# Second DFT stage of a long convolution: 128x128 products with a block-diagonal matrix, or 64x64 products on the four parts of the array

## The chip, the cores and the metric

The kernel runs on one core of a Trainium2 chip. TensorE (PE in the profile) multiplies, VectorE (DVE), ScalarE (ACT) and GpSimd (POOL) work on tiles, SyncE (SP) issues transfers. The metric is the device time of one execution in microseconds; the median of three runs before the change is 216.64 us (216.44 to 218.06).

## What is computed

`x` is `A_q`, 2048 positions of 640 channels. Cut to what matters:

```python
xn = layernorm(x)
k_shift = sum over t of k shifted by t, times shift_k       # 4 taps
kv = k_shift * v
y  = irfft(rfft(kv padded to 4096) * rfft(ssm_k padded to 4096))[:2048]
y  = y + kv * ssm_D
s  = xn * y
g  = silu(gelu(xn @ w1 + b1) @ w2 + b2)                     # 640 -> 1728 -> 640
out = x + s * g
```

So there are two branches: a causal convolution of length 2048 in each of 640 channels, with a filter of its own, and a dense layer pair. Both use the normalized `x`, and they meet in a product.

## The kernel before

**The convolution** is done by a DFT in two stages, both as products on TensorE. Position s is 16 p + n, with p on the 128 partitions and n = 0 to 15. Stage one (`k_f1` for the filter, `u_f1` for kv) multiplies, for each n, a table of 128 cosines or sines by the 128x640 tile of that n; the result, 128 lines of real and 128 of imaginary parts, is copied from PSUM to SBUF and stored to scratch in HBM (scrK, scrU; GpSimd's queue). Read back in another order (SyncE's queue), 32 groups of 128 lines each arise. A group holds four frequencies r; for each it has 16 values of n, each with a real and an imaginary line. Stage two is a DFT over n: one constant 128x128 matrix, `F2m`, with four equal 32x32 blocks on its diagonal and zeros elsewhere. The filter goes through it in `k_f2` (steps `ff0` to `ff31` of the list), kv in `u_f2` (`mu0` to `mu31`).

`product` (`mp`, L532) is VectorE's: it multiplies a kv group, read straight from PSUM, by the filter's group and by the same group with its real and imaginary lines exchanged (`swap_load`, a transfer from SBUF to SBUF). The inverse of stage two, `inv1` (`mc`, L541 and L542), multiplies these two results by the constant matrices `I1a` and `I1b`, both with the same four diagonal blocks' places, and adds them in PSUM. The result is copied out (`me`), stored to scrC (`ms`), read back (`yl`), and goes through the inverse of stage one (`y`, L573); then come the gate, the addition of `x` and the store.

A product of a group is two matmuls of 320 columns each, since a bank of PSUM holds 512 floats: `mm2` (L196) writes the halves of the 640 channels to two neighbouring banks. `mm2` serves both stages; the trace tells them apart by the operand (`mats` is stage two). Copies out of PSUM are `evac`, on ScalarE (L190) or VectorE (L191).

**The dense layers** (`ffn1`, L439, steps `h` and `ha`/`hb`; `ffn2`, L454, steps `g`) run over four chunks of 512 positions. They depend only on `x`, and are laid between the convolution's steps.

**The order** is written out by hand, or by a planner outside the kernel: `PLAN` is a list of 957 words, and the kernel issues them one by one, in the order of each engine. A word gives the step, the row of the shared SBUF tile `mem` after "/", the PSUM banks after "@" (all eight banks are handed out this way), and the engine of a copy after "~": `me2/74~a` copies inverse 2 to row 74 on ScalarE, `~d` means VectorE. No scheduler changes this order; a step waits until its operands are there, and all later steps of the same engine wait behind it.

Of the kernel before, what the change touches and what calls it, by code (L numbers as in the profile page):

```python
# [36 lines left out]
cm1_1/32 he0_1 h0_8@7 cm0_1/89 he0_13 he0_11 kl2 cm1_0/58 h0_7@1 kl3 he0_8 cm0_0/60 tt1_0@0 cm0_2/62 he0_7 xl2/91
g0_1@2 ca1_1 te1_0/0~d vl1/4 cm0_3/95 g0_0@3 ge0_1/0 ca0_1 vl2/97 d ca0_2 kt4@4 ge0_0/1 cm1_3/101 kt1@5 kc4/103~a
g0_2@2 vl3/104 gm0_0 kc1/108~a ca0_3 gm0_1 cm1_2/109 kt0@3 ge0_2/2 kt2@6 cv0 kc0/68~a kf1_0@0.1 kf1_1@4.5 ke1_0/66~a
g0_5@7 gm0_2 kc2/65~d ke1_1~a ca1_2 ks1 cm2_0/32 kf0_0@2.3 ge0_5/1 kt7@6 cm2_1/34 ke0_0/89~a kf0_1@0.1 kf2_1@4.5  # L40
cm2_2/62 kt3@7 ke0_1~a kf2_0@2.3 kc3/64~d ks0 kf4_1@0.1 ke2_0/36~a kc7/95~d kt5@7 ke2_1~a ca2_1 kf4_0@2.3 g0_3@6
kc5/96~a ks2 gm0_5 cm2_3/28 ke4_0/108~a ke4_1~d kf5_1@4.5 ca2_2 ge0_3/0 kt6@7 ks4 kf3_0@2.3 kf5_0@0.1 gm0_3
ke3_0/34~a g0_6@6 cm3_1/65 ke5_0/67~a ca2_3 kc6/38~a ke5_1~d kt8@2 ge0_6/2 kf6_0@0.1 cv2 ks5 kf6_1@4.5 kf3_1@6.7
ke6_0/39~a kc8/110~d g0_4@3 ke3_1~d ke6_1~a cm3_0/62 ks3 ks6 cm3_2/89 uf0_0@0.1 ge0_4/1 uf0_1@6.7 tt1_1@2 ue0_0/28~a
ca1_3 uf1_1@4.5 tt1_2@3 ue0_1~a te1_1~d uf1_0@0.1 te1_2~a kf8_0@6.7 us0 cv1 g0_7@2 ue1_0/4~a ue1_1~d ke8_0/37~a
cm3_3/108 us1 uf2_0@0.1 gm0_6 ge0_7/0 uf2_1@4.5 gm0_4 uf3_0@6.7 ue2_0/101~a cm4_0/60 it1@3 ue3_0/67~a kt9@2 ue2_1~d
kf8_1@0.1 kc9/96~a kf7_0@6.7 ie1~d kf7_1@4.5 us2 ke7_0/30~a it2@2 ke8_1~d it3@3 ke7_1~a kf9_1@6.7 ie2/39~d ks8 ie3~a
kf9_0@0.1 uf3_1@4.5 st2_2 ks7 h1_0@2 ue3_1~a ke9_0/34~d us3 kt10@3 ke9_1~a uf4_0@4.5 kc10/36~d kt11@0 he1_0 ks9
ue4_0/28~d h1_1@1 kc11/64~d kf10_0@6.7 ca3_1 kf11_0@4.5 he1_1 h1_3@3 ke10_0/4~d ke11_0/95~a ca3_2 uf4_1@0.1 he1_3
uf5_0@6.7 kf10_1@4.5 cm4_3/58 ue4_1~a kt12@2 h1_6@3 ue5_0/101~a ca3_3 us4 kc12/103~a ke10_1~d kf11_1@0.1 uf5_1@6.7  # L50
he1_6 h1_2@2 ke11_1~d ks10 ue5_1~a cv3 ks11 kf12_0@4.5 he1_2 kf12_1@0.1 us5 kt13@3 ke12_0/37~d ke12_1~a uf6_1@6.7
h1_11@2 cm4_2/67 kc13/110~a ks12 cm4_1/65 kf13_0@4.5 he1_11 uf6_0@0.1 h1_4@3 ke13_0/89~d ue6_0/35~a ca4_1 ue6_1~a
kf13_1@4.5 uf7_0@0.1 he1_4 st2_3 us6 uf7_1@6.7 kt15@2 ke13_1~a h1_5@3 st2_0 kc15/34~a ks13 ue7_0/108~a h1_9@4 ca4_2
he1_5 st2_1 kf15_0@0.1 ue7_1~a kf15_1@2.3 kt14@5 ke15_0/32~a us7 h1_8@6 ca4_3 kc14/43~a rs2 ke15_1~d he1_9 h1_10@7
cv4 he1_8 kf14_0@0.1 he1_10 cm5_1/4 kf14_1@2.3 ks15 uf8_0@4.5 ke14_0/6~a h1_7@6 nm2_1 nm2_2 ke14_1~a nm2_0 uf8_1@0.1
nm2_3 he1_7 ks14 uf9_0@2.3 ue8_0/95~d h1_13@7 ue8_1~a ue9_0/101~d us8 tt2_2@6 he1_13 uf9_1@4.5 cm5_0/62 h1_12@0
ue9_1~a gm0_7 fl2/64 ca5_1 fl3/66 us9 tt2_0@1 he1_12 fl5/89 g1_1@7 cm5_2/37 fl0/58 te2_0/12~a fl15/16 cm5_3/18
fl14/20 te2_2~a ca5_2 g1_0@6 ge1_1/2 cm6_2/97 ca5_3 cm7_1/43 ff5@2.3 ge1_0/1 ff4@4.5 ff6@0.1 cv5 fl1/22 fe4/108~a
g1_6@7 fe5~a gm1_0 cm6_1/24 fe6/26~a mk2/60 cm6_0/28 uf10_0@4.5 ge1_6/0 uf10_1@2.3 cm7_0/6 uf11_0@0.1 ue10_0/30~a
g1_3@6 ue10_1~a ca6_1 ue11_0/95~a us10 ca7_1 ca6_2 uf11_1@4.5 ge1_3/1 ff2@2.3 ff3@0.1 ue11_1~a cm7_2/45 g1_5@7 fl6/0  # L60
fe2/2~a us11 cm6_3/4 fe3~a ca7_2 mk1/18 ff7@4.5 ca6_3 ff0@2.3 fe7~a ff1@0.1 g1_2@6 fl7/102 cm7_3/37 fe0/35~a fl4/33
mk3/64 cv6 fe1~a gm1_3 mk0/52 ca7_3 uf12_0@4.5 ge1_5/1 uf13_0@2.3 ue12_0/100~a uf12_1@0.1 st3_1 g1_4@7 ue13_0/24~a
cv7 ue12_1~a gm1_1 us12 gm1_5 uf15_0@4.5 ge1_2/2 st3_3 uf13_1@2.3 ge1_4/1 uf15_1@0.1 ue13_1~a tt2_1@6 ue15_0/22~d
g1_7@7 te2_1~a us13 gm1_2 st3_0 uf14_0@2.3 ue15_1~d ge1_7/2 uf14_1@4.5 h2_9@6 ue14_0/4~a st3_2 us15 ue14_1~a
ff12@0.1 he2_9 gm1_6 us14 ff8@2.3 gm1_4 ff28@4.5 fe12/58~d h2_7@7 rs3 fe28/37~d h2_0@0 fe8/62~a gm1_7 he2_7 ml1/104
nm3_3 ff10@4.5 ml7/106 nm3_0 ff30@2.3 he2_0 ff9@6.7 nm3_2 ml3/95 h2_12@1 fe30/28~a fe10/30~d ml0/97 ml2/43 fe9~a
nm3_1 fl9/45 ff14@2.3 he2_12 ff31@4.5 ml5/47 ff29@6.7 mk4/99 h2_8@0 fe14/49~a fe29~d fe31~a fl12/6 ff11@2.3 he2_8
q1/66 mu2@6.7 ff15@4.5 mp2/24 fe11~a h2_3@1 fl8/70 fe15~a mu7@2.3 he2_3 fl13/32 mu0@4.5 mp7/72 mc2@6.7 h2_1@0 mk5/22
me2/74~a mp0/4 mu6@6.7 mk7/76 he2_1 ff18@2.3 h2_11@1 fe18/78~a mp6/101 ml6/20 ff19@4.5 he2_11 mu3@2.3 fl10/16 h2_5@0
fe19~a mp3/89 fl11/103 ff24@6.7 he2_5 ff25@4.5 h2_13@1 fe24/96~d fe25~a mk14/24 mc0@2.3 he2_13 mu4@6.7 me0/34~d  # L70
mc3@4.5 ml9/51 h2_10@0 mp4/45 me3~a mk9/64 ms1 ff17@2.3 he2_10 ff16@4.5 h2_6@1 q3/2 fe16/26~a fe17~d mk15/6 ff27@6.7
he2_6 ff26@4.5 mc4@2.3 fe26/18~d fe27~a h2_4@0 me4/89~d mc6@4.5 he2_4 ff20@6.7 me6/70~a ff21@2.3 fe20/32~d h2_2@1
fe21~d ff22@4.5 he2_2 q2/12 ff13@6.7 mu15@2.3 fe22/45~a g2_2@0 mp15/74 fe13~a mu1@4.5 ge2_2/0 mu5@6.7 mp1/101
ml15/16 mc7@2.3 ml4/0 g2_3@1 me7~a mp5/107 mk6/43 ms3 mu10@4.5 ge2_3/1 mu11@2.3 gm2_2 mk10/72 mc5@6.7 mp10/60 g2_5@0
me5~a ml8/109 gm2_3 ms2 mp11/47 mc10@6.7 ge2_5/2 mc1@4.5 gm2_5 me10/107~a mk8/60 mu8@0.1 me1~d g2_4@2 mp8/22 ms0
mu13@6.7 ge2_4/0 mu9@4.5 mp13/30 mc8@0.1 ml14/70 g2_1@3 me8/101~a mp9/98 mu14@0.1 ge2_1/1 ff23@6.7 gm2_4 mk13/0
mc9@4.5 gm2_1 fe23~a g2_0@2 mp14/89 me9~a q0/103 ml11/21 ms4 mk11/62 mu12@6.7 ge2_0/2 mc11@4.5 gm2_0 tt3_0@3 ml10/34
me11~a mp12/98 tt3_2@2 mc14@0.1 ms5 mc13@4.5 me14/76~a te3_0/47~d mk12/89 mc12@6.7 te3_2~a mu16@0.1 me12/43~d
tt3_1@3 me13~a g2_6@2 mp16/58 te3_1~a ms6 mc16@6.7 ge2_6/0 mc15@4.5 gm2_6 me16/30~a mu17@0.1 me15~a h3_7@3 mp17/98
ml13/100 ms7 mu18@6.7 mu19@4.5 g2_7@2 mp18/107 ml12/58 mp19/74 mc18@0.1 ge2_7/1 mu27@6.7 he3_7 h3_0@2 gm2_7  # L80
me18/109~d mc19@4.5 mp27/26 he3_0 mu20@0.1 h3_5@3 me19~a mp20/60 ms9 mu21@6.7 he3_5 mu24@4.5 h3_10@2 mp21/43
mc20@0.1 he3_10 h3_4@3 mp24/51 me20/107~a mc21@6.7 he3_4 mu26@0.1 me21~d mc24@4.5 h3_6@2 mp26/64 me24/101~a ms10
mu22@6.7 he3_6 mc17@4.5 mp22/79 mu23@0.1 me17~a h3_9@3 ms8 mp23/77 mc22@4.5 he3_9 mu25@6.7 me22/35~a h3_8@2 mp25/75
mu28@0.1 he3_8 mc23@4.5 mc25@6.7 me23~a mp28/109 h3_3@3 me25~a ms11 mu30@4.5 ms12 he3_3 mu29@6.7 mp30/43 mc26@0.1
h3_2@2 me26/95~a mp29/0 mc30@0.1 he3_2 mu31@4.5 me30/51~a h3_1@3 mp31/107 mc27@6.7 he3_1 mc28@0.1 me27~d mc31@4.5
me28/45~d ms13 mc29@2.3 me31~a h3_13@6 me29~d ms15 h3_11@7 ms14 he3_13 h3_12@6 he3_11 he3_12 g3_1@7 yl6/89 yl15/58
yl13/60 yl12/62 g3_4@6 ge3_1/2 yl10/64 yl7/101 yl4/99 yl2/6 y6@0.1 gm3_1 ge3_4/0 g3_0@7 gm3_4 yc6 yt6 yo6 yl0/0
y13@4.5 os6 ge3_0/1 y12@2.3 gm3_0 yc13 g3_7@6 yc12 yt13 yl3/95 yt12 yo12_1 yl5/97 yo12_0 y10@0.1 ge3_7/2 os12 y4@4.5
gm3_7 yc10 y7@2.3 yc4 yt10 y15@6.7 yc7 yo10 yl1/107 y2@0.1 yt4 os10 yc15 g3_3@4 yt7 yl9/109 yc2 yo4 yl14/43 yo7 os4
yt2 os7 yt15 yl11/89 y3@2.3 ge3_3/0 yo2 yl8/45 y0@6.7 yo15_1 yc3 gm3_3 g3_2@5 os15_1 yo13_1 yc0 yt3 os2 yo3 yt0 os3  # L90
yo0 y5@0.1 ge3_2/1 y1@2.3 os0 gm3_2 yc5 yo13_0 y9@6.7 yc1 os13 yt5 y14@4.5 yc9 yo5 g3_5@0 yt1 os5 yc14 yt9 yo1 yo9
# [566 lines left out]
```

## Time and profile before

| | |
|---|---|
| median of the runs | 216.64 us |
| the profiled execution | 215.17 us, its span 213.4 us |
| mean granted TensorE clock | 0.995 |
| TensorE busy | 201.4 us (94%), 1417 matmuls recorded, 1429 weight loads |
| VectorE, ScalarE, GpSimd busy | 182.0, 151.6, 41.3 us |
| `ffn1` L439 / `ffn2` L454 | 298 and 448 matmuls recorded, 66.1 and 65.7 us |
| L196 with `mats` (stage two) | 128 matmuls, 23.6 us in the groups |
| L541 + L542 (its inverse) | 64 + 64 matmuls, 18.0 + 18.0 us in the groups |
| L532 (`product`, VectorE) | 32, 46.3 us, 1485 ns each |
| HBM | 33.76 MB read, 18.35 MB written |

The profile is one execution. Busy times in the groups are unions of the group's records, and matmuls overlap in the array, so the mean of 299 ns of a 320-column matmul is the time from its start to its modelled end, not the distance to the next one. The view of windows gives busy us of each engine in a stretch of the span. The page's slices are fortieths of the span, 5.3 us each, in tenths.

### The profile page before, as it was taken

Reading aid. Unit: us, or ns where it says so; the run is one execution under the profiler, and the core shown is the slowest. Engines: PE = TensorE matmul, PEld = TensorE weight load, DVE = VectorE, ACT = ScalarE, POOL = GpSimd, SP = SyncE. Lnnn points to the kernel's source line nnn. Section 1 sums busy time; section 2 is a strip of 40 time slices with the busy share of each in tenths; the row PEclk is TensorE's granted clock in tenths of the full one; section 3 lists DMA queues with packets and bytes.
Section 4 is the critical chain, followed back from the end, with each engine's and each line's share of the span. In section 5 each row is a group of like instructions: output and inputs, shape, how many; then the busy total and the mean of one; then the engine's idle time right before and its main releaser. Section 6 shows DMA issues by size and latency. Waiting matters only on the chain.

```text
span 213.4 us, 4003 instructions
## 1 busy us (share of the span) xinstructions
PE 201.4 (94%) x1417; PEld 132.2 (62%) x1429; DVE 182.0 (85%) x307; ACT 151.6 (71%) x235; POOL 41.3 (19%) x72
## 2 busy tenths in 40 slices
PE   3999999999999999999998999999999999979992
...
PEclk9999999999999999999999999999999999999998
...
GB/s 217 315 391 371 368 414 410 418 285 203 217 155 300 158 159 279 369 225 296 188 222 342 389 372 366 346 281 190 372 206 61 62 138 49 205 335 361 380 271 112
DMA packets 27114, 57.62 MB, mean 270 GB/s; under 512 B 2966, under 2 KB 16983, under 8 KB 27094
## 3 DMA queue, kind: packets, MB, share of 16 engines
...
HBM read 33.76 MB, written 18.35 MB: 244 GB/s over the span
## 4 chain that ended last, share of the span: by engine, by line
PE 65%; DMA 19%; DVE 6%; SPq 3%; issue 2%; ACT 1%; POOL 1%; DVEq 0%; POOLq 0%
PE ps L454 21%; PE ps L439 17%; PE ps L196 13%; DMA mem<-in_A_k_dram 8%; DMA mem<-scrK 7%; PE ps L542 4%; PE ps L541 4%; DMA mem<-scrC 3%; PE ps L573 3%; DVE mem L490 3%; DMA skp<-in_A_shift_k_dram 2%; DVE mem L493 2%; PE ps L471 2%; PE ps L420 1%; SPq L523 1%
## 5 line engine op out<-in xcount | busy, mean ns | idle before, releaser
L190 ACT CAST mem<-ps 128x640 bf16<-128x640 f32 x92 | 60.7, 698 | 9.7 <-PE ps L542 5.6
L439 PE MATMUL ps<-mem,w_sb 128*128 128x512 bf16 (+1 forms) x298 | 66.1, 358 | 0.6
L454 PE MATMUL ps<-w_sb,hT 128*128 128x320 bf16 x448 | 65.7, 299 | 0.0
L454 PEld LDWEIGHTS <-hT 128*128 128x128 bf16 x448 | 43.6, 98 | 16.8
L532 DVE TENSOR_TENSOR mem<-ps,mem 128x1280 bf16<-128x1280 f32 x32 | 46.3, 1485 | 4.8 <-PE ps L196 3.6
L444 ACT ACTIVATE hT<-ps,b_f 128x512 bf16<-128x512 f32 (+1 forms) x56 | 37.1, 693 | 12.5 <-PE ps L439 11.6
L439 PEld LDWEIGHTS <-w_sb 128*128 128x128 bf16 x310 | 30.1, 98 | 24.0
L191 DVE CAST mem<-ps 128x640 bf16<-128x640 f32 x36 | 28.9, 816 | 6.4 <-PE ps L196 3.6
L459 ACT ACTIVATE sl<-ps 128x320 bf16<-128x320 f32 x32 | 14.1, 439 | 27.6 <-PE ps L454 24.7
L490 DVE TENSOR_TENSOR mem<-mem 128x1280 bf16<-128x1280 bf16 x32 | 25.1, 815 | 0.1
L196 PE MATMUL ps<-mem,mats 128*128 128x320 bf16 x128 | 23.6, 299 | 1.4 <-DMA mem<-scrK 1.1
L548 POOL DMA_DIRECT2D scrC<-mem x16 | 11.7, 732 | 64.0 <-ACT mem L190 50.2
L196 PE MATMUL ps<-mem 128*128 128x320 bf16 x128 | 22.8, 299 | 0.0
L493 DVE TENSOR_TENSOR mem<-mem 128x1280 bf16<-128x1280 bf16 x24 | 19.2, 811 | 0.0
L463 DVE TENSOR_TENSOR mem<-mem,sl 128x320 bf16<-128x320 bf16 x32 | 9.9, 318 | 10.4 <-ACT sl L459 10.3
L196 PEld LDWEIGHTS <-mats 128*128 128x128 bf16 x128 | 12.2, 98 | 10.0 <-DMA mem<-scrK 2.1
L541 PE MATMUL ps<-mem,mats 128*128 128x320 bf16 x64 | 18.0, 299 | 0.0
L542 PE MATMUL ps<-mem,mats 128*128 128x320 bf16 x64 | 18.0, 299 | 0.0
L190 ACT COPY mem<-ps 128x640 bf16<-128x640 bf16 (+2 forms) x22 | 15.9, 746 | 1.5 <-PE ps L414 1.5
L506 POOL DMA_DIRECT2D scrU<-mem x16 | 8.7, 542 | 36.1 <-ACT mem L190 33.5
L196 PEld LDWEIGHTS <-mem 128*128 128x128 bf16 x128 | 12.0, 98 | 5.8 <-issue 0.4
L484 POOL DMA_DIRECT2D scrK<-mem x16 | 9.0, 564 | 26.5 <-ACT mem L190 17.2
...
## 6 DMA issues: line engine op xcount, KB each, us to landing
...
```

What stands on the lines that cost most here:

```text
L190: return nc.scalar.copy(out=out_ap, in_=in_ap)
L191: return nc.vector.tensor_copy(out=out_ap, in_=in_ap)
L196: nc.tensor.matmul(out=o[:, h, :], lhsT=lhsT, rhs=rhs[:, h * HALF:(h + 1) * HALF], start=start, stop=stop)
L439: nc.tensor.matmul(out=bank(hname(c, ft))[:, a:b], lhsT=w1_sb[:, t, ft * P:(ft + 1) * P], rhs=rhs, start=(t == 0), stop=(t == DT - 1))
L444: nc.scalar.activation(out=hT[0:M, ft, :], in_=bank(hname(c, ft))[0:M, :], func=ACT.Gelu_apprx_tanh, bias=b1_f[0:M, ft:ft + 1], scale=1.0)
L454: nc.tensor.matmul(out=bank(f"g{c}_{i}")[:, 0:HALF], lhsT=hT[0:M, ft, q * P:(q + 1) * P], rhs=w2_sb[0:M, ft, hs], start=(ft == 0), stop=(f ...
L459: nc.scalar.activation(out=at["sl", c, i], in_=bank(f"g{c}_{i}")[:, 0:HALF], func=ACT.Silu)
L490: nc.vector.tensor_tensor(out=rows(f"cm{i}_{j}", 2), in0=rows("klh", 2, 3 + 2 * i - j), in1=taps(j), op=ALU.mult)
L493: nc.vector.tensor_tensor(out=rows(f"cm{i}_0", 2), in0=rows(f"cm{i}_0", 2), in1=rows(f"cm{i}_{j}", 2), op=ALU.add)
L532: nc.vector.tensor_tensor(out=rows(f"mp{g}", 2).rearrange("p k (h c) -> p k h c", h=2), in0=banks(f"mu{g}")[:, None, :, :].to_broadcast([P ...
L541: nc.tensor.matmul(out=o[:, h, :], lhsT=I1a, rhs=row(f"mp{g}", ia)[:, hs], start=True, stop=False)
L542: nc.tensor.matmul(out=o[:, h, :], lhsT=I1b, rhs=row(f"mp{g}", ib)[:, hs], start=False, stop=True)
```

## The change

A new helper, `mm4`, takes the place of `mm2` in `k_f2` and `u_f2`, and of the four matmuls in `inv1`. It cuts the 128x128 matrix to its two 64x64 blocks on the diagonal and makes four matmuls: for each half h of the channels and each half q of the input lines, the block of q times those 64 lines, written to the 64 output lines of half q (h = 0) or of the other half (h = 1). So each of the four uses another quarter of the array. In the second half of the channels the lines of a group come out with their halves exchanged, in the filter and in kv alike; the inverse exchanges them back.

The number of words, 957, and of steps of each kind is the same. In the program, TensorE gets 256 matmuls and 256 weight loads more.

```diff
+    def mm4(name, m, rhs, start=True, stop=True):
+        o = banks(name)
+        for h in range(2):
+            for q in range(2):
+                i, j = slice(64 * q, 64 * q + 64), slice(64 * (q ^ h), 64 * (q ^ h) + 64)
+                nc.tensor.matmul(out=o[j, h, :], lhsT=m[i, i], rhs=rhs[i, h * HALF:(h + 1) * HALF], start=start, stop=stop)
...
     def k_f2(g):
-        mm2(f"ff{g}", F2m, row(f"fl{g // 2}", g % 2))
+        mm4(f"ff{g}", F2m, row(f"fl{g // 2}", g % 2))
...
     def u_f2(g):
-        mm2(f"mu{g}", F2m, row(f"ml{g // 2}", g % 2))
+        mm4(f"mu{g}", F2m, row(f"ml{g // 2}", g % 2))
...
     def inv1(g):
-        o = banks(f"mc{g}")
         ia, ib = at["p", g]
-        for h in range(2):
-            hs = slice(h * HALF, (h + 1) * HALF)
-            nc.tensor.matmul(out=o[:, h, :], lhsT=I1a, rhs=row(f"mp{g}", ia)[:, hs], start=True, stop=False)
-            nc.tensor.matmul(out=o[:, h, :], lhsT=I1b, rhs=row(f"mp{g}", ib)[:, hs], start=False, stop=True)
+        mm4(f"mc{g}", I1a, row(f"mp{g}", ia), stop=False)
+        mm4(f"mc{g}", I1b, row(f"mp{g}", ib), start=False)
```

The list is a new one throughout. Its beginning, old and new, and a stretch of stage two of the new one:

```diff
-io1/0 dm qs xl0_0/8 cl0/12 id pd/28 xl0_1 klh/35 qr wa0 wa1 w wa2 io2 wu@0 xl1/54 wb0 st0_0 ws1/58 kl0 mh st0_1 cl2
-pt@1 em0@2 pb sq0 em1@3 rc0 wb1 nm0_0 nm0_1 tx0@4 st0_2 tx1@5 te0_0/65~a wv5 st0_3 te0_1~a cl4 ee0/69~a ha1@6 ee1~d
...
+io1/0 dm qs xl0_0/8 cl0/12 id pd/28 wa0 xl0_1 klh/35 qr wa1 w xl1/54 io2 wu@0 cl2 cl1 st0_0 ws1/58 mh cl4 st0_1 pt@1
+em0@2 pb sq0 em2@3 rc0 cl3 nm0_0 nm0_1 tx0@4 wa2 st0_2 tx1@5 te0_0/65~a wv2 te0_1~a st0_3 kl0 ee0/69~a ha3@6 ha2@7
...
+mu12@0.1 mc11@6.7 mp13/12 g2_5@2 ml11/103
+me11~d mp12/89 mc14@4.5 ms5 ge2_5/2 mu16@6.7 tt3_0@3 me14/14~a g2_6@2 te3_0/39~a gm2_5 mk12/109 mp16/97 mc12@4.5
```

In the new list the filter's transposes and first stage (`kt`, `kf`) stand earlier, the warming run `wv` has two matmuls instead of five, the 165 copies out of PSUM are split anew (41 on VectorE, 124 on ScalarE; before 51 and 114), and rows, banks and the order of transfers are given out anew. Steps of stage two and its inverse stand in 39 runs of one to three steps between other TensorE steps; in the old list there are 36 such stretches of one to four.

More of the change, by code (lines that the diff above doesn't have):

```diff
@@ L31 @@
 PLAN = """
-io1/0 dm qs xl0_0/8 cl0/12 id pd/28 xl0_1 klh/35 qr wa0 wa1 w wa2 io2 wu@0 xl1/54 wb0 st0_0 ws1/58 kl0 mh st0_1 cl2
-pt@1 em0@2 pb sq0 em1@3 rc0 wb1 nm0_0 nm0_1 tx0@4 st0_2 tx1@5 te0_0/65~a wv5 st0_3 te0_1~a cl4 ee0/69~a ha1@6 ee1~d
-ha0@7 sq1 ws0/73 rc1 em2@1 nm0_2 cl3 nm0_3 em3@0 ee2~d tx2@4 tx3@5 ha3@2 te0_2~d s ha2@3 ha5@1 te0_3~a ha4@4 cl1
-ee3~a hb5 hb4 ws2/77 h0_9@5 xl3/81 st1_0 h0_12@0 st1_1 ss he0_4 hb1 st1_2 hb0 hb3 st1_3 hb2 he0_0 sm it0@4 he0_3 rs1
-h0_10@7 ie0/85~d he0_2 he0_9 h0_6@4 he0_12 kz nm1_3 vl0/28 nm1_1 he0_10 h0_13@5 nm1_0 he0_6 nm1_2 he0_5 h0_11@0 kl1
@@ L37 @@
[L37 to L91, printed above, removed]
@@ L92 @@
-os1 yt14 y8@2.3 os9 ge3_5/2 yo14_0 y11@6.7 gm3_5 yc8 yo14_1 g3_6@1 yc11 os14 yt8 yo8 yt11 os8 yo11 ge3_6/0 os11
-gm3_6 yo15_0 os15_0
+io1/0 dm qs xl0_0/8 cl0/12 id pd/28 wa0 xl0_1 klh/35 qr wa1 w xl1/54 io2 wu@0 cl2 cl1 st0_0 ws1/58 mh cl4 st0_1 pt@1
+em0@2 pb sq0 em2@3 rc0 cl3 nm0_0 nm0_1 tx0@4 wa2 st0_2 tx1@5 te0_0/65~a wv2 te0_1~a st0_3 kl0 ee0/69~a ha3@6 ha2@7
+sq1 ws0/73 rc1 em3@2 nm0_2 ha0@1 nm0_3 xl3/77 ee3~d ha5@0 ha1@4 s tx2@5 tx3@2 wb0 te0_3~a te0_2~a em1@2 wb1 ws2/81
+hb3 st1_2 hb0 xl2/85 hb1 ee1~d hb5 ss st1_1 hb2 he0_1 vl0/89 h0_7@5 st1_0 h0_6@2 kl1 st1_3 he0_2 he0_3 ha4@4 d sm
@@ new lines @@
+rs1 he0_6 kt1@7 hb4 kc1/93~d ee2~a kt0@6 kl2 h0_11@2 he0_4 kc0/28~d kz nm1_0 he0_0 nm1_1 kf1_0@6.7 he0_11 nm1_3
+h0_10@3 nm1_2 kl3 he0_5 ke1_0/29~d h0_9@4 he0_7 cm1_2/31 he0_10 kf0_1@0.1 vl3/58 cm1_0/33 he0_9 kf0_0@6.7 kf1_1@2.3
+cm0_1/62 ke0_0/94~a h0_13@5 ke1_1~a ke0_1~d kt2@4 he0_13 ks1 h0_12@6 cm0_2/96 ks0 cm0_0/98 h0_8@7 he0_12 kc2/64~d
+ca0_1 kf2_0@2.3 he0_8 kt4@6 ke2_0/0~d kt3@0 kc4/100~a kf2_1@4.5 ca0_2 kc3/2~a kf4_1@2.3 kf4_0@6.7 ke2_1~d kt6@1
+ke4_0/3~a kt10@0 kc6/5~d ks2 kf3_1@4.5 kc10/6~a vl1/107 kf3_0@6.7 cm0_3/105 kt5@1 vl2/101 ke4_1~a g0_3@0 cm1_1/67
@@ new lines @@
+kc5/7~a ks4 ca0_3 ke3_0/65~a ke3_1~a ca1_1 kf5_0@2.3 it0@1 ge0_3/0 ks3 cm1_3/62 it2@6 kf5_1@4.5 ca1_2 g0_1@7
+ie2/93~a ie0/35~d gm0_3 ca1_3 ke5_0/28~a kf6_1@0.1 ke5_1~a cv0 kf6_0@2.3 kt8@6 ge0_1/1 ks5 it1@4 cv1 ke6_0/105~a
+g0_0@5 kc8/97~a ie1~d ke6_1~a st2_1 ks6 uf0_0@2.3 cm2_2/67 ge0_0/2 uf1_0@6.7 kt7@4 ue0_0/0~a uf0_1@0.1 st2_3 it3@5
+ue1_0/30~a g0_2@2 kc7/100~a st2_2 ue0_1~a ie3~a st2_0 us0 kf7_1@6.7 kf7_0@0.1 ge0_2/0 cm2_0/62 kt9@3 rs2 ke7_0/89~a
+uf2_0@4.5 g0_4@2 cm2_1/2 ke7_1~a kc9/7~a gm0_0 ca2_1 ks7 ue2_0/4~a nm2_0 uf2_1@0.1 ge0_4/2 kf8_0@6.7 nm2_1 kf8_1@4.5
@@ new lines @@
+ue2_1~a gm0_4 g0_5@3 nm2_2 us2 nm2_3 ca2_2 ke8_0/91~a cm2_3/64 kf9_0@0.1 ke8_1~a uf1_1@6.7 gm0_1 tt1_0@2 ge0_5/2
+ca2_3 ks8 g0_6@4 ue1_1~a cm4_2/28 te1_0/0~a us1 cv2 ke9_0/105~a gm0_2 kf9_1@6.7 ge0_6/1 cm3_0/32 kt11@5 ke9_1~a
+uf3_0@2.3 uf3_1@0.1 kc11/100~d tt1_1@4 ue3_0/97~a ks9 cm3_2/67 uf4_0@6.7 ue3_1~a tt1_2@5 kf10_0@2.3 gm0_5 te1_2~d
+ue4_0/39~a us3 uf5_1@0.1 cm3_1/64 kt15@5 ke10_0/89~a g0_7@6 gm0_6 kc15/66~a st3_2 te1_1~a ca3_1 kf11_0@2.3 ge0_7/0
+kf10_1@4.5 cm4_0/107 kt14@7 ke11_0/4~a h1_2@6 kc14/99~a cm4_1/91 ke10_1~a ca3_2 uf5_0@2.3 h1_12@7 he1_2 ks10
@@ new lines @@
+ue5_0/30~d uf4_1@4.5 ue5_1~d kt13@2 h1_0@3 cm3_3/105 ue4_1~a us5 he1_12 ca4_1 kt12@6 us4 h1_1@0 he1_0 ca3_3
+kf11_1@4.5 cm5_0/97 he1_1 h1_6@1 ke11_1~d kc12/34~a h1_9@7 cv3 he1_6 ks11 cm4_3/64 uf6_0@4.5 he1_9 uf6_1@0.1 h1_5@3
+ue6_0/6~d ue6_1~a cm5_1/67 us6 kf12_1@6.7 he1_5 kf12_0@4.5 ca4_2 kf14_0@0.1 ke12_0/62~a h1_7@3 ke12_1~d kc13/89~a
+ca4_3 ke14_0/90~a h1_10@4 ks12 he1_7 cm5_2/105 kf13_0@6.7 he1_10 h1_11@5 gm0_7 cm6_2/12 ke13_0/14~a ca5_1 kf14_1@0.1
+he1_11 h1_8@4 cv4 ke14_1~a uf7_0@2.3 ca5_2 ks14 he1_8 uf9_1@6.7 uf9_0@0.1 ue7_0/109~a cm6_0/39 h1_13@5 ue9_0/41~a
@@ new lines @@
+ue9_1~d kf15_0@2.3 he1_13 kf13_1@0.1 cm5_3/43 us9 kf15_1@6.7 ke13_1~a h1_4@4 ke15_0/4~d ke15_1~a ks13 ca5_3
+uf7_1@0.1 he1_4 ks15 uf8_0@2.3 h1_3@5 cm6_1/6 ue7_1~a ue8_0/16~a cv5 us7 uf8_1@6.7 tt2_0@4 he1_3 ca6_1 uf10_0@0.1
+ue8_1~a uf11_0@2.3 g1_7@5 cm6_3/99 ue10_0/62~a us8 fl4/64 ca6_2 fl7/67 ue11_0/101~a fl0/18 te2_0/20~a st3_1 fl3/24
+uf10_1@6.7 fl1/26 uf11_1@0.1 fl2/28 ue10_1~a g1_4@2 ca6_3 ge1_7/2 us10 ue11_1~d cv6 us11 ff8@6.7 ff9@0.1 ge1_4/1
+tt2_1@3 st3_0 fl14/89 fe8/91~a uf12_0@4.5 g1_2@2 fe9~a st3_3 ue12_0/30~a mk4/41 te2_1~a cm7_1/43 rs3 uf12_1@6.7
@@ new lines @@
+cm7_0/45 ge1_2/0 uf13_0@0.1 uf13_1@4.5 ue12_1~a g1_5@3 cm7_2/0 ue13_0/2~a us12 ca7_1 ue13_1~a cm7_3/47 us13 ff6@6.7
+ff7@0.1 ff0@4.5 ca7_2 fe6/4~a g1_3@2 fl11/6 fe0/32~a nm3_2 ca7_3 fe7~a gm1_2 mk3/12 nm3_1 ff4@6.7 ge1_5/0 ff5@4.5
+gm1_4 ff14@0.1 fe4/58~a cv7 g1_1@3 fl5/14 fe5~a nm3_3 nm3_0 ge1_3/1 mk2/16 fe14/97~d uf14_1@6.7 gm1_5 uf14_0@4.5
+gm1_3 uf15_0@0.1 ge1_1/0 gm1_7 g1_0@2 ue14_0/39~a gm1_1 ue14_1~d ue15_0/69~a us14 uf15_1@4.5 ge1_0/1 ff1@6.7 ff2@0.1
+ue15_1~a tt2_2@3 gm1_0 fl6/24 fe2/71~d g1_6@2 fe1~a us15 te2_2~d mk0/0 ff3@4.5 ge1_6/2 ff22@0.1 ff15@6.7 fe3~d
```

27 lines of the change are left out of this document (added).

## The prediction

> **What bounds the kernel now.** I read the page's shares of busy time first, then the slices of the span, then busy time by stage, and last the TensorE timeline inside the second DFT stage.
>
> ```profile
> PE 201.4 (94%) x1417; PEld 132.2 (62%) x1429; DVE 182.0 (85%) x307; ACT 151.6 (71%) x235; POOL 41.3 (19%) x72
> ...
> PE   3999999999999999999998999999999999979992
> ...
> PEclk9999999999999999999999999999999999999998
> ```
>
> TensorE (PE) is busy in 201.4 of 213.4 us at the full granted clock. Its 12 idle us lie in the first slice, in the last, and around the turn to the last stage (36th slice). Everywhere else the order of products on TensorE is the time: a product that becomes cheaper moves all behind it forward until another engine is late.
>
> The stage that the change touches, by the view of windows (84.8 is the first second-stage product, 180 the end of the last inverse; the last row is the tail):
>
> ```profile
> 84.80:111.00 26.20, 25.55 (x175) 16.80 (x177) 23.28 (x46) 21.69 (x36) 4.54 (x8) 1.00 0.73 259
> 111.00:156.00 45.00, 44.10 (x305) 28.84 (x306) 35.46 (x36) 27.45 (x44) 5.84 (x8) 1.00 0.96 333
> 156.00:180.00 24.00, 23.89 (x148) 14.36 (x148) 22.85 (x20) 15.09 (x23) 3.69 (x6) 1.00 0.27 96
> 180.00:213.40 33.40, 27.91 (x193) 18.35 (x191) 18.57 (x46) 17.61 (x29) 2.18 (x3) 0.97 0.76 266
> ```
>
> Columns are the stretch, its length, then busy us of PE, weight loads, VectorE (DVE), ScalarE (ACT) and POOL, then clock, DMA share, GB/s. Over 95.2 us TensorE idles 1.66. But DMA share is 0.96 in the middle row, and VectorE has 22.85 of 24.00 in the third: two limits stand right behind TensorE.
>
> What a product costs is not its mean of 299 ns in the groups (the modelled latency) but the distance between starts, here in an inverse:
>
> ```profile
> 120.91 0.30 PE L541 MATMUL ps<-mem,mats 128*128 128x320 bf16 x1
> 121.05 0.30 PE L542 MATMUL ps<-mem,mats 128*128 128x320 bf16 x1
> ...
> 121.19 0.30 PE L541 MATMUL ps<-mem,mats 128*128 128x320 bf16 x1
> 121.19 0.10 PEld L542 LDWEIGHTS <-mats 128*128 128x128 bf16 x1
> 121.32 0.30 PE L542 MATMUL ps<-mem,mats 128*128 128x320 bf16 x1
> ```
>
> Starts lie 0.41/3 = 136 ns apart. The next weights load while a product runs (121.19 beside 121.19), so the loads cost nothing.
>
> **The change, part by part.** Per group, `k_f2` and `u_f2` make two products of 320 columns and `inv1` four: 32 x (2 + 2 + 4) = 256 products, x 136 ns = 34.8 us. In the new form each pair of products becomes four of 64x64, one on each quarter of the array. That is 128 sets of four; 256 products and 256 weight loads more are issued.
>
> *A set of four, itself.* No quarter product is in the trace, so bounds. If the four stream at once, a set takes one pass, 136 ns. If they run one after another, 4 x 136 = 544 ns. Between these stand the four weight loads. The nearest row of a slower load is that of the filter transposes: L471's loads read with a stride, take 147 ns in the groups instead of 98, and then pace the products:
>
> ```profile
> 37.37 0.47 PE L471 MATMUL ps<-ident,mem 128*128 128x128 bf16 x5
> 37.68 0.71 PE L196 MATMUL ps<-mem 128*128 128x320 bf16 x4
> ```
>
> Five in 0.31 us are 62 ns each, where the chain has twelve of L420 with fast loads in 0.67 us, 56 ns each. A load of half as many columns at that slow rate is 31 ns (an estimate), four are 124 ns, just under 136: hidden. At the whole 62 ns, four would be 248. I take 136, since the loads hide in every row of this stage: 128 x (272 - 136) = **-17.4 us**. Ends: -17.4 and +34.8.
>
> The row shows loads issued during products on the same array rows. The Trainium skill, "TensorE: Matmul & The Clock Gate", section "Part 3: Packing small matmuls — row/col tiling", says that a load overlaps products in flight only when its row group differs; by that, the third and fourth product of each set (same row halves as the first two) would start a pass later and a set would cost 272 or more, no gain at all. Its other branch, a load into the background weight buffer, is what the 128x128 rows here agree with.
>
> *Going in and out of the four-part form.* Sets stand in the new list in 39 runs of one to three steps (3.3 sets on average; the old list has 36 such stretches), between products of the whole array: 78 changes of form. The trace has one such change: the transpose of a 19-row tile, between full ones.
>
> ```profile
> 6.42 0.10 PEld L347 LDWEIGHTS <-prm 19*128 19x128 bf16 x1 [1.30 <-DVE stats L393]
> 6.45 0.17 PE L347 MATMUL ps<-ident,prm 19*128 19x19 bf16 x1 [0.43 <-DMA prm<-in_A_ssm_D_dram]
> 6.55 0.34 PEld L339 LDWEIGHTS <-skp 128*128 128x128 bf16 x4
> 6.55 0.50 PE L339 MATMUL ps<-ident,skp 128*128 128x128 bf16 x3
> ```
>
> The next load and product start 0.10 us after the small product started, not after its modelled 0.17, so a change costs at most about 0.10 us there. The upper bound is a full emptying: the latency 299 - 136 = 163 ns, plus an exposed load of 98 = 261 ns. I take 0.10, the one row that shows a change: 78 x 0.10 = **+7.8 us** (0 to 20.4). On entering a run, three of the four loads are not covered: 3 x 31 ns x 39 = **+3.6 us** (0 to 7.3 at 62 ns).
>
> The Trainium skill, "TensorEngine Tiling (Array Packing)", section "Key Properties", says that a change of tiling form empties the array. By that alone, at 261 ns, the sum would be 12.6 us higher; the row above allows no more than 0.10 but is one change behind a product of 19 columns.
>
> Behind a change wait TensorE's next products, and behind those the copies and GELUs that read their banks.
>
> *Copies.* Ten copies out of PSUM go from VectorE to ScalarE: 51 on VectorE and 114 on ScalarE become 41 and 124. At 816 and 698 ns (L191, L190) VectorE has 8 us less, ScalarE 7 us more. ScalarE is 71% busy and covers it, at no cost; without that cover each late copy is 0.7 us. VectorE's relief is what lets its 32 products (L532, 1485 ns, 46.3 us) keep up if the stage shrinks.
>
> *The list.* Filter transposes and first-stage products of the filter come earlier (after 15.6 us of TensorE work instead of 28.8), stores and loads change places, and a run of five warming products becomes two (0.65 us less). In TensorE work, the first second-stage product stands at 78.1 us as against 77.8, and behind the last inverse lie 26.1 us as against 27.2. The tail waits for the round trip through scrC anyway (5.5 idle us in the fourth window), so I count neither. POOL issues the same 48 stores, SyncE the same scratch loads in another order. At the start, the five filter loads end after 5.73 MB on SyncE's list; at the 261 and 377 GB/s of the first two 10 us they land at about 18.3 us, and TensorE comes to them at 13.0 + 4.8 idle = 17.8 us: half a us either way.
>
> *Waits taking the place.* Before 180 us the stage would go from 95.2 to about 89; its VectorE work from 81.6 us to some 76 (6 to 7 of the copies fall here), 85% as before; its DMA from 69 us of work at 72% to 77%, with the middle window near full. For late transfers, and the start, I add **+1.0 us** (0 to 3).
>
> Sum: 213.4 - 17.4 + 7.8 + 3.6 + 1.0 = 208.4 us span. The profiled execution took 215.17, 1.8 more than its span, so 210.2; the median of the runs, 216.64, is 1.5 above that. **Forecast 211.6 us**, 2.3% faster. About 1% is what a measurement of this kernel can tell from no change.
>
> **Rivals.**
> - *Emptying the array eats the gain (slower).* Place: 78 changes. Price: 261 ns each, the latency of L541 plus its load. It decides from (17.4 - 3.6 - 1.0)/78 = 0.16 us on. Sum 213.4 - 17.4 + 20.4 + 3.6 + 1.0 = 221.0 span, **224 us**. For: the next load can't go ahead over the change. Against: the 0.10 of the 19-row row.
> - *Weight loads pace the sets.* At 248 ns a set the gain is 3.1 us; with 7.8 and 1.0 (the entry is then in the pace) the span is 219.1, **222 us**; at 190 ns, **215 us**. For: 62 against 56 ns at L471. Against: no load of this stage shows.
> - *The four do not run at once*, the change doesn't do what it says: two after two is 272 ns, and 213.4 + 7.8 + 1.0 gives **225 us**; all four in turn, 34.8 more, **260 us**. Nothing in the trace speaks for or against.
> - *Changes nearly free:* 30 ns each, no load exposed: 213.4 - 17.4 + 2.3 + 1.0, **203 us**. VectorE at 76 us would still fit in that stage (81 us).
> - *DMA becomes the bound:* the middle window's 0.96 x 45 = 43.3 us of transfers don't shrink, while its TensorE work falls to about 40: 3 us lost instead of 1.0, **214 us**.
>
> **How the numbers follow.** Chances: forecast (207 to 214) 0.42; changes nearly free 0.08; DMA 0.06; weight loads 0.16 (a fifth of it faster, a third about even); emptying 0.20; not at once 0.08. Faster by over 1% (under 214.5): 0.42 + 0.08 x 0.9 and small parts of DMA and loads, 0.5; slower (over 218.8): 0.36; between: 0.14. The range goes from near the free case to the emptying one, 205 to 224; what runs in turn, and the very lowest, are left out. The likeliest case alone is 207 to 214.
>
> **What would show it.** Right: starts of sets about 0.14 us apart within a run, four products starting almost together; the first product of a run and the first after it about 0.10 us late; TensorE's work in the stage down by some 6 us; the first second-stage product still near 85 us; the tail still some 33 us. Wrong: gaps of 0.2 us or more at each change, sets 0.2 us and more apart inside a run, the four starting one by one, or VectorE or DMA waits of more than a us between inverses.

## The result

The changed kernel takes 210.0 us (median of four runs, 208.12 to 211.18), the kernel before 217.0; the ratio is 0.966 (95% interval 0.958 to 0.975). Beside later runs of the kernel before, on other occasions, it came out at 0.974 (0.970 to 0.979) and 0.968 (0.963 to 0.973). So the change is worth 2.5 to 3.5%; the forecast was 211.6 us, 2.3%. The profiled execution took 211.18 us, its span 209.4. Ratios leave out the few executions that lie more than 1.5% above the fastest of their kernel; medians include them.

The page of the changed kernel (line numbers behind the helper are 8 higher, in `inv1` and after it 5 higher):

```profile
PE 193.4 (92%) x1682; PEld 116.2 (55%) x1682; DVE 175.1 (84%) x297; ACT 158.3 (76%) x245; POOL 43.0 (21%) x72
...
PE   2878998999999999989998999989999999969992
...
PEclk9999999999999999999999999999999999999999
```

TensorE is busy 8.0 us less, VectorE 6.9 us less, ScalarE 6.7 us more: the ten copies went over as the list says. But eight slices of TensorE are thinner than before: the first four, the 7th, the 18th, the 27th and the 36th.

By stage, the view of windows of the changed kernel (89.8 us is the first second-stage product, 176.9 the end of the last inverse; columns as in the prediction):

```profile
0.00:24.00 24.00, 17.24 (x132) 12.02 (x133) 19.46 (x60) 17.69 (x22) 8.35 (x20) 1.00 0.96 339
24.00:60.00 36.00, 35.16 (x300) 25.24 (x299) 35.67 (x67) 32.70 (x55) 11.20 (x17) 1.00 0.83 322
60.00:89.80 29.80, 28.72 (x183) 16.84 (x180) 29.70 (x48) 27.78 (x44) 7.55 (x14) 1.00 0.48 175
89.80:110.00 20.20, 20.16 (x190) 12.40 (x191) 15.37 (x32) 15.68 (x26) 4.40 (x6) 1.00 0.90 318
110.00:152.00 42.00, 40.47 (x428) 20.76 (x424) 33.83 (x35) 27.54 (x46) 4.31 (x6) 1.00 0.98 350
152.00:176.90 24.90, 24.90 (x277) 11.04 (x275) 23.10 (x19) 19.76 (x31) 5.70 (x8) 1.00 0.31 108
176.90:209.40 32.50, 26.74 (x190) 17.90 (x186) 18.00 (x45) 17.14 (x29) 1.43 (x2) 0.98 0.76 274
```

and the part ahead of stage two in the kernel before, which was not shown:

```profile
0.00:24.00 24.00, 19.70 (x142) 13.23 (x145) 21.36 (x61) 19.04 (x24) 9.34 (x20) 1.00 0.96 331
24.00:60.00 36.00, 35.54 (x302) 25.81 (x302) 35.75 (x62) 27.86 (x46) 7.82 (x14) 1.00 0.83 327
60.00:84.80 24.80, 24.68 (x164) 14.84 (x163) 24.70 (x42) 22.86 (x37) 7.87 (x14) 1.00 0.54 200
```

The span's gain of 4.0 us is a balance. Stage two and its inverse take 87.1 us instead of 95.2, 8.1 less. The tail takes 32.5 instead of 33.4, 0.9 less. The part ahead of stage two takes 89.8 instead of 84.8, 5.0 **more**, with nearly the same products in it (78.1 and 77.8 us in the prediction's count). By 24 us TensorE has been busy 2.5 us less than before and VectorE 1.9 less. Ahead of stage two TensorE waits 3.7 us in both kernels for the identity matrix that GpSimd builds; besides this the view of waits names 0.8 us of its waits in the kernel before

```profile
PE ps L347 <- DMA prm<-in_A_ssm_D_dram: 0.4, 1, 0.4
PE ps L471 <- DVE mem L191: 0.4, 1, 0.4
```

and 5.0 us in the changed kernel, of which these are the longest (the first at 16.2 us, the second just ahead of stage two, the third at 7 us):

```profile
PE ps L347 <- ACT mem L190: 1.4, 1, 1.4
PE ps L204 <- DMA mem<-scrK: 1.1, 1, 1.1
PE ps L355 <- DMA prm<-in_A_ssm_D_dram: 1.0, 1, 1.0
```

So 4.2 us of the delay are waits that have a name. VectorE is full from 24 us to stage two in both kernels (35.67 of 36 and 29.70 of 29.80 here), and by the start of stage two it has done 84.8 us of work where it had done 81.8 before. Being late at 24 us explains only a part: in another profile of the changed kernel (`after_beside`) VectorE is 0.8 us behind there, not 1.9, and stage two still begins 4.2 us late.

**What a set costs.** In the chain of work that ended last, pieces in order of time (start, us, what):

```profile
162.38 1.19 PE ps L447 x5
163.57 0.67 PE ps L204 x16
164.23 1.19 PE ps L447 x5
```

```profile
152.70 2.01 PE ps L462 x14
154.71 0.80 PE ps L204 x20
155.51 1.19 PE ps L447 x5
```

Sixteen quarter products, four sets, take 0.67 us; twenty, five sets, 0.80. One set more is 0.13 us, what the full product of 320 columns costs. The rest, 0.67 - 4 x 0.136 = 0.13 us, is paid once per run, and the five products L447 behind or ahead of a change take 1.19 us where the chain of before had 1.08: 0.11 more. The starts of single instructions in the trace are finer. The four products of a set start within 10 ns. Sets follow at 135 to 136 ns. From the last full product to the first set it is 309 ns where full products of 512 columns follow at 216 (25 cases), 231 where those of L462 change to others at 140 (11 cases), 228 behind a product of L196 where these follow at 136, and 150 where transposes follow at 56 (one case each): 91 to 94 ns for going in, the same behind 512, 320 and 128 columns. From the start of the last set to the next full product it is 238 (35 of 39 cases) instead of 136: 102 ns for going out. The second set of a run starts 160 ns after the first, not 136. These 24 ns fit weight loads that nothing covers, though no run shows that by itself. Together 219 ns per run. So 128 sets x 136 + 39 runs x 219 = 26.0 us, against 34.8 before: 8.9 us won, less 0.5 to 2.1 us (three profiles) in which a run waits for its data.

### The profile page after: what moved, and what is told of

The parts are those of the page before. It is cut to its first block, busy times and chain, and to the rows that moved or that the text cites. A ratio compares the mean times of both kernels' runs of the same rounds, so it can differ in the third digit from the quotient of the medians.

```text
span 209.4 us, 4487 instructions
## 1 busy us (share of the span) xinstructions
PE 193.4 (92%) x1682; PEld 116.2 (55%) x1682; DVE 175.1 (84%) x297; ACT 158.3 (76%) x245; POOL 43.0 (21%) x72
## 4 chain that ended last, share of the span: by engine, by line
PE 56%; issue 18%; DMA 14%; DVE 6%; ACT 2%; SPq 1%; POOL 1%; POOLq 0%; ACTq 0%
PE ps L462 18%; PE ps L447 18%; PE ps L196 7%; DMA scrC<-mem 5%; PE ps L204 5%; PE ps L578 4%; DMA mem<-in_A_q_dram 4%; DMA mem<-scrK 2%; DMA mem<-scrC 2%; DVE mem L191 2%; PE ps L428 2%; PE ps L479 2%; DVE mem L498 1%; ACT mem L190 1%; PE ps L558 1%
## 5 line engine op out<-in xcount | busy, mean ns | idle before, releaser
L447 PE MATMUL ps<-mem,w_sb 128*128 128x512 bf16 (+1 forms) x310 | 68.5, 360 | 0.7 <-DMA w_sb<-in_B_w_dram 0.5
L190 ACT CAST mem<-ps 128x640 bf16<-128x640 f32 x98 | 64.7, 700 | 4.5 <-DMA mem<-mem 1.2
L462 PE MATMUL ps<-w_sb,hT 128*128 128x320 bf16 x448 | 65.9, 299 | 0.0
L462 PEld LDWEIGHTS <-hT 128*128 128x128 bf16 x448 | 42.8, 98 | 18.1 <-issue 2.0
L447 PEld LDWEIGHTS <-w_sb 128*128 128x128 bf16 x310 | 27.9, 98 | 29.2 <-issue 6.9
L191 DVE CAST mem<-ps 128x640 bf16<-128x640 f32 x30 | 24.1, 820 | 5.4 <-PE ps L204 3.5
L204 PE MATMUL ps<-mem,mats 64*64 64x320 bf16 x512 | 25.5, 304 | 2.6 <-DMA mem<-scrK 1.1
L196 PE MATMUL ps<-mem 128*128 128x320 bf16 x128 | 23.6, 299 | 0.8 <-DVE mem L191 0.6
L204 PEld LDWEIGHTS <-mats 64*64 64x64 bf16 x512 | 11.9, 105 | 18.4 <-issue 13.4
L190 ACT COPY mem<-ps 128x640 bf16<-128x640 bf16 (+2 forms) x26 | 20.2, 806 | 2.4 <-PE ps L422 1.8
L196 PEld LDWEIGHTS <-mem 128*128 128x128 bf16 x128 | 12.0, 98 | 8.1 <-DVE mem L191 1.5
L401 DVE BATCH_NORM_STATS2 stats<-mem 128x6 f32<-128x320 bf16 x32 | 13.8, 472 | 1.4 <-DMA mem<-in_A_q_dram 1.4
L582 ACT CAST mem<-ps 128x640 bf16<-128x640 f32 x16 | 10.2, 700 | 2.4 <-PE ps L578 2.0
```

Source lines behind the costliest of these rows:

```text
L190: return nc.scalar.copy(out=out_ap, in_=in_ap)
L191: return nc.vector.tensor_copy(out=out_ap, in_=in_ap)
L196: nc.tensor.matmul(out=o[:, h, :], lhsT=lhsT, rhs=rhs[:, h * HALF:(h + 1) * HALF], start=start, stop=stop)
L204: nc.tensor.matmul(out=o[j, h, :], lhsT=m[i, i], rhs=rhs[i, h * HALF:(h + 1) * HALF], start=start, stop=stop)
L401: nc.vector.bn_stats(out=stats[:, n, h, :], in_=x_row(n)[:, h * HALF:(h + 1) * HALF])
L447: nc.tensor.matmul(out=bank(hname(c, ft))[:, a:b], lhsT=w1_sb[:, t, ft * P:(ft + 1) * P], rhs=rhs, start=(t == 0), stop=(t == DT - 1))
```

## The experiments

All ratios are to the kernel before, run on the same chip beside them.

**The new list with the old products.**

```diff
-        mm4(f"ff{g}", F2m, row(f"fl{g // 2}", g % 2))
+        mm2(f"ff{g}", F2m, row(f"fl{g // 2}", g % 2))
```

and likewise in `u_f2` and `inv1`.

> The new list with the old 128x128 products in stage two and its inverse. Theory A (the gain is that of the products; in the changed kernel's trace a set of four costs 136 ns, a run in the four-part form 219 ns on top, so 128 x 136 - 39 x 219 = 8.9 us of TensorE time are won): 210.0 + 8.9 less up to 3 us of waits for data that the slower products cover, so 216 to 219 us, level with the kernel before (217.0). Rival B (the new list brings at least half of the gain by its order and the ten copies moved to ScalarE): 213.5 us or less.

Measured: 217.0 us beside 215.76, ratio 1.009 (1.005 to 1.012). Theory A held, rival B fell: the order and the moved copies bring nothing by themselves, and cost 0.9%. Stage two begins at 89.1 us here too, so the late start belongs to the list, not to the products. Beside this kernel the four-part products bring 7.2 us on the same list (217.0 and 209.84 us, on the same chip), of the 8.9 us counted.

**The old list with the new products.** The edit is the reverse: the three functions as in the changed kernel, `PLAN` as in the kernel before.

> The old list with the four-part products. It has 36 stretches of stage-two steps. Theory A: TensorE wins 128 x 136 - 36 x 219 = 9.5 us; the old list's own waits for transfers (DMA share 0.96 in its middle window) give 1 to 3 us back: 217.0 - 9.5 + 2 = 209.5 us (207.5 to 211), as fast as the changed kernel. Rival B (the gain needs a list laid out for it, since VectorE or the transfers are late in the old one): 213.5 us or more. In the old list VectorE keeps ten more copies, 8 us; its last window before 180 us had 22.85 of 24.00 us busy, so B would show there.

Measured: 213.37 us beside 215.76, ratio 0.989 (0.985 to 0.992). That lies just under the rival's line: of 9.5 us of TensorE time only 2.4 arrive. Theory A fell. Stage two begins at 84.8 us, as in the kernel before. Neither half of the change gives more than 1.2% alone (1.009 x 0.989 = 0.997), both together 2.5 to 3.5%.

**Two parts of the array at once instead of four.**

```diff
-                i, j = slice(64 * q, 64 * q + 64), slice(64 * (q ^ h), 64 * (q ^ h) + 64)
+                i, j = slice(64 * q, 64 * q + 64), slice(64 * q, 64 * q + 64)
```

> The changed kernel, but both halves of the channels go through the two quarters on the diagonal of the array: output lines 64 q to 64 q + 63 for both h, so that only two of the four products of a set can run at once. The result stays the same. Theory A (the four really share one pass): a set becomes 2 x 136 = 272 ns, starts of the third product 136 ns behind the first; 128 x 136 = 17.4 us more TensorE time, less 2 to 4 us of waits that are covered: 222 to 227 us. Rival C (products with the same input lines run one behind the other already in the changed kernel): no difference within 1%, 208 to 212 us.

Measured: 226.0 us beside 215.76, ratio 1.049 (1.043 to 1.056), so 16 us above the changed kernel. Theory A held. The chain shows sets of twice the length, five in 1.48 us instead of 0.80 (0.27 us each and the same fixed rest):

```profile
182.80 1.48 PE ps L204 x20
184.28 1.19 PE ps L447 x5
```

So the crossing `q ^ h`, which sends the two halves of the channels to different output lines, is where the gain sits. With blocks on the diagonal alone a set takes 0.27 us, as long as the two full products that it replaces, and the changes of form come on top: 39 x 0.219 = 8.5 us, where this kernel takes 9.0 us more than the new list with the old products.

**The four-part form in stage two alone, not in its inverse.** `k_f2` and `u_f2` as changed, `inv1` as in the kernel before.

> The changed kernel with the old 128x128 products in the inverse only (32 x 4 matmuls); stage two of the filter and of kv stay in the four-part form. In the second 320 channels the two halves of a group's lines are not exchanged back, so these channels come out permuted; the work is the same. Sets in the four-part form fall from 128 to 64, but they still stand in 37 runs. Theory A (a fixed price per run of 219 ns): the gain shrinks to 64 x 136 - 37 x 219 = 0.6 us, so 8.3 us more than the changed kernel less up to 3 us of covered waits, 215 to 218 us. Rival D (the change of form costs nothing by itself, each set brings its share): half of the gain stays, 213.5 us or less.

Measured: 216.36 us beside 215.76, ratio 1.004 (1.000 to 1.007). Theory A held, D fell: half of the sets keep nothing of the gain against the kernel before, since they stand in nearly as many runs. Beside the new list with the old products (217.0) it is 0.6 us less, what the sum for theory A gives. The chain of this kernel shows the price on products that are otherwise the old ones:

```profile
140.70 0.40 PE ps L204 x8
141.09 0.24 PE ps L549
...
141.47 0.14 PE ps L549
141.61 0.14 PE ps L550
```

Two sets take 0.40 us, 0.13 above 2 x 0.136, and the product at 141.09, the first full one behind them, has 0.24 us instead of 0.14.

**Why the products bring so little on the old list.** Two edits of `PLAN` in that kernel, alone and together. In the first the nine inverse copies on VectorE go to ScalarE (each `me..~d` becomes `me..~a`):

> The old list with four-part products, and the nine copies of the inverse that it gives to VectorE moved to ScalarE (9 x 0.82 = 7.4 us of VectorE). The question is why four-part products alone won only 1.1% on the old list although they take 9.5 us off TensorE. Theory V (VectorE is then the pace: 33.3 of its us fall in 156 to 180 us and before, 23.29 of 24.00 in that window): most of the gain comes back, 209 to 211 us where the kernel before takes 215.8. Rival T (the transfers of the old list come too late; its longest TensorE waits there name scrU and scrK): within 1% of the 213.4 us without the edit.

In the second the loads `q1`, `q3`, `q2`, `q0` go behind `mp18`, `mp27`, `mp21`, `mp24`:

> The old list with four-part products, and the four loads of x for the final addition (4 x 640 KB, steps q0 to q3) moved from about 115 to 135 us to about 158 to 165 us, where the DMA share is 0.3. Theory T (transfers pace stage two in the old list): 2.6 MB, some 7 us of full transfer rate, leave the window with a DMA share of 0.93 to 0.96; 209.5 to 211.5 us. Rival V (VectorE paces it): within 1% of 213.4 us.

Measured: 212.44 us beside 215.56, 0.988 (0.985 to 0.992), and 212.50 us, 0.987 (0.982 to 0.993). Neither moves the ratio from 0.989. Theories V and T both fell as single causes, T less firmly: the four loads, which are issued at 113 to 146 us in the unedited kernel, were issued at 150 to 154 us, not at 158 to 165, so the DMA share from 111 to 156 us was still 0.91.

> The old list with four-part products, the nine copies of the inverse on ScalarE and the four loads of x late, both edits at once; each alone left the time within 1 us of the 213.4 us without it. Theory (VectorE and the transfers are both close behind TensorE in the old list, and taking one away only shows the other): most of the 9.5 us come, 209 to 211 us. Rival (the old order of the steps itself holds stage two back, since it lays each product just ahead of data that come no earlier): 211.5 us or more.

Measured: 212.53 us beside 216.2, ratio 0.981 (0.977 to 0.985). That is the rival's side of the line. It is 0.7% below the 0.989 of the products alone, but the unaltered changed kernel also stood 0.6% lower on this occasion (0.968) than on the one before (0.974), so it is not shown that the two edits together give anything. Windows and groups of the kernel with both (its list is one line shorter, so its line numbers are one lower):

```profile
84.80:111.00 26.20, 24.93 (x212) 15.05 (x213) 23.85 (x47) 21.39 (x37) 4.51 (x8) 1.00 0.74 263
111.00:156.00 45.00, 42.57 (x465) 22.61 (x471) 34.97 (x34) 29.93 (x50) 5.88 (x8) 1.00 0.91 306
156.00:178.00 22.00, 19.53 (x217) 8.38 (x214) 18.12 (x14) 17.28 (x27) 4.24 (x6) 1.00 0.46 174
```

```profile
L539 DVE TENSOR_TENSOR mem<-ps,mem 128x1280 bf16<-128x1280 f32 x32 | 46.6, 1487 | 7.6 <-PE ps L203 5.8 <-ACT mem L189 1.1 <-issue 0.7
...
L203 PE MATMUL ps<-mem,mats 64*64 64x320 bf16 x512 | 26.8, 305 | 4.8 <-DVE mem L539 1.7 <-DMA mem<-scrU 1.0 <-ACT mem L189 0.9
```

In the last window no engine is full, and no transfer rate: VectorE has 18.12 of 22.00 us, DMA 0.46. Yet TensorE idles 6.2 us in these 93.2 us, where it idled 1.66 in the 95.2 us of stage two before. By the view of waits its products wait there for VectorE's products (L539) 1.7 us, for reads from scrU and scrK 1.9 and for a copy 0.9; VectorE waits for TensorE 5.8. In the changed kernel TensorE waits for VectorE 0.8 us and VectorE for TensorE 4.7. A reading that fits is that the old order lays `mu`, `mp` and `mc` of a group, and several `mc` behind each other, at the distance that suits products of twice the length, so that they wait for each other in turn; no run shows it, and scratch reads that come late are a rival as large. By the starts of the weight loads, ten of its 36 runs last 0.1 to 1.1 us longer than the shortest run with as many sets, 4.7 us in all; in the changed kernel it is three runs and 2.1 us, and in two other profiles of it 0.8 and 0.5 us. Two long runs of the inverse (`mc14 mc13 mc12 mu16`, `mc27 mc28 mc31 mc29`) have no shorter one to compare with; at 136 ns a set each is 0.5 us too long. Which moves of the old list would remove these waits was not tried.

**The late start.** Two edits of the new list ahead of stage two:

```diff
-id pd/28 wa0 xl0_1 klh/35
+id pd/28 xl0_1 wa0 klh/35
...
-us11 ff8@6.7 ff9@0.1 ge1_4/1 tt2_1@3 st3_0 fl14/89 fe8/91~a uf12_0@4.5 g1_2@2 fe9~a st3_3 ue12_0/30~a mk4/41 te2_1~a
+us11 ge1_4/1 tt2_1@3 st3_0 fl14/89 uf12_0@4.5 ff8@6.7 ff9@0.1 ue12_0/30~a te2_1~a g1_2@2 fe8/91~a fe9~a st3_3 mk4/41
```

> The changed kernel with two edits ahead of stage two: the first load of w1 goes behind the second half of the first x chunk (as in the old list), and the first two stage-two products stand behind the transposes tt2_1 and the product uf12_0 instead of ahead of them, so that these cover 0.7 us of the wait for scrK. In the changed kernel stage two begins 4.3 to 5.0 us later than in the kernel before, with the same TensorE work ahead of it; some 2 us of this arise by 17 us, after x's second half landed late, 1.1 to 1.8 us at the wait for scrK. Theory H (these waits are the loss): stage two begins 1.5 to 2.5 us earlier and the end follows: 1.5 to 2.5 us less than the changed kernel. Rival (the wait for scrK grows by what the start wins, since the stores set it, or the tail waits longer): within 0.7 us of the changed kernel.

> The changed kernel once more, unaltered, beside the same runs of the kernel before as the next three. Both theories: about 0.966 of the kernel before, 208 to 210 us where that takes 215.8.

Measured: 208.52 us (0.969, 0.965 to 0.973) beside the changed kernel's 209.84 (0.974, 0.970 to 0.979): 1.3 us less, between the two theories, and the intervals overlap. Two windows of the head, and the first second-stage product:

```profile
0.00:24.00 24.00, 18.07 (x136) 12.38 (x138) 20.28 (x62) 18.61 (x23) 9.51 (x20) 1.00 0.95 341
24.00:60.00 36.00, 35.63 (x305) 25.83 (x305) 35.63 (x68) 33.27 (x54) 10.03 (x16) 1.00 0.85 330
```

```profile
89.37 0.47 PE L203 MATMUL ps<-mem,mats 64*64 64x320 bf16 x8 [1.45 <-DMA mem<-scrK]
```

The first edit did what it should: VectorE's statistics of x's second half start at 8.1 us, as in the kernel before, where they start at 9.8, 10.1 and 8.6 us in three profiles of the changed kernel. But little of it reaches stage two. TensorE is done with the work ahead at 87.9 us and waits 1.4 us for scrK, so that stage two begins at 89.4 us: 0.5 us earlier than in the profile shown above, behind 0.7 us of work that used to follow, and inside the 89.1 to 91.1 us of the changed kernel's three profiles. VectorE's busy time by 24 us, 20.28 us, is 0.8 above that profile's and 0.3 below another's. Theory H fell in its place: of the late start 4.5 us remain against the kernel before, and TensorE's named waits ahead of stage two are still 3.7 us where that one has 0.8.

**Transfers in stage two of the new list.** The mended head, and `q3`, `q0`, `q2`, `q1` behind `ml14`, `mu21`, `mu23`, `mu26`:

> The mended head, and the four loads of x for the final addition moved from about 118 to 128 us (in the changed kernel's list) to about 158 to 165 us. In the changed kernel the window from 110 to 152 us has a DMA share of 0.96 to 0.98, and TensorE waits there for transfers that feed stage two, 1.5 to 3 us. Theory T (the transfers are the next limit of stage two): 1 to 2.5 us less than the mended head, 206 to 207.5 us where the kernel before takes 215.6. Rival V (VectorE's products, which are 80% of that window, take the place): within 0.7 us of the mended head, 208 to 209 us.

> The changed kernel, unaltered, beside the two others and the same runs of the kernel before: 0.966 to 0.974 of the kernel before, 208 to 210 us, in both theories.

Measured: 208.19 us (0.962, 0.958 to 0.966) beside 209.67 (0.968, 0.963 to 0.973). That is 0.994 of the changed kernel, as with the mended head alone. The four loads were issued at 147 to 154 us, not at 158 to 165. Its middle window:

```profile
110.00:152.00 42.00, 40.53 (x433) 21.35 (x436) 34.49 (x34) 28.15 (x46) 4.31 (x6) 1.00 0.89 298
```

The DMA share fell from 0.96 in the mended head to 0.89 (344 and 298 GB/s, 1.9 MB less in 42 us), and TensorE's busy time hardly changed (40.15 us there, 40.53 here). Theory T's 1 to 2.5 us do not show. But the mended head alone did not run on this occasion, and with intervals of about 0.4% to each side a gain of 1 us could hide. Single reads that come late are not excluded either: TensorE still waits 1.1 us for scrU. The two kernels with the mended head are the fastest tried, each some 0.6% below the changed one; the intervals overlap.

## Why the prediction was right, point by point

**What bounds the kernel** was right for stage two: TensorE cheaper, stage shorter. It was not the whole truth ahead of stage two, where VectorE is as full as TensorE and TensorE's waits went from 0.8 to 5.0 us.

**A set at 136 ns** was right to the nanosecond, and `two_at_once` shows why. The sentence of the Trainium skill ("TensorE: Matmul & The Clock Gate", "Part 3: Packing small matmuls — row/col tiling") that a load overlaps only products of other row groups does not fit: sets follow each other at 136 ns with four loads in each, onto the input lines of products that still run, and not at the 272 that the prediction worked out from it.

**The change of form at 0.10 us** was right: 91 to 94 and 102 ns, so 39 x 0.195 = 7.6 us where the sum had 7.8. Its basis, one row behind a product of 19 columns, carried, because the price hardly depends on the product ahead. The Trainium skill's rule in "TensorEngine Tiling (Array Packing)", section "Key Properties", that a change of form drains the array, fits a fixed price; the emptying itself shows in no run. The rival that took the full latency and an exposed load for it, 261 ns, was 2.7 times too dear.

**Uncovered loads on entering a run** were mis-sized: 24 ns per run measured (if these are the loads), not 93, so 0.9 us and not 3.6. The slow strided load (62 ns) was not the right neighbour. Of TensorE time in the stage, then, 6.0 us were forecast and 8.9 came.

**"I count neither"** for the new list ahead of stage two was wrong, and it is the step that failed. Its TensorE work is nearly the same, as computed, but stage two began 4.2 to 6.2 us later, not near 85 us. The estimate followed the filter loads only ("half a us either way"). What came in its place are waits of TensorE, 5.0 us against 0.8 in the profiled execution: among them 1.4 us at 16 us for a ScalarE copy and 1.1 us (up to 2.0 in other profiles) for scrK. `list_alone` puts them down to the list. The second half of the first x chunk, late behind a weight load on SyncE's queue, is a small part: with it early, stage two began 0.5 us earlier. What sets the rest stays open.

**+1.0 us of waits** in the stage did not come: TensorE idles 1.57 us in its three windows, 1.66 before. The tail's 0.9 us, counted at nothing, were won; the new list has 1.1 us less TensorE work there (26.1 and 27.2 in the prediction).

So the total was near by luck, because errors stood against each other: in the profiled execution 5.0 us too little in the head, 3.1 too much in the stage (95.2 - 6.0 + 1.0 = 90.2 forecast, 87.1 measured) and 0.9 in the tail; the span came out at 209.4 where the sum had 208.4. **Of the rivals**, weight loads as the pace, products in turn, and a change at 261 or at 30 ns are excluded by the starts. For DMA as the bound, `head_and_q` shows no gain from 1.9 MB less in the middle window. Not among them was what the two single halves showed: that on the old list the cheaper product is worth 1.1%, with two edits there 1.9% at most, and on the new one 3.4%.
